# Decode attention over a long key cache: keys transposed as fp32 words, queries computed in row form, and the last output weights loaded in one piece

## The chip, the cores and the metric

One Trainium2 chip, of which one core is used. The time is device microseconds of one execution, the median of several runs. Six runs of the kernel before gave 390.95 to 393.68 us, median 391.86. The profile is of one further execution, which took 392.09 us.

A core has five engines that run their own instruction streams and wait for each other by semaphores: TensorE (PE) for matrix products, its weight loads shown apart as PEld; VectorE (DVE) and ScalarE (ACT) for elementwise work; GpSimd (POOL); and SyncE (SP), which here only issues loads. Sixteen DMA engines move data between the device memory (HBM) and the on-chip buffer. PE writes to PSUM, eight banks of 2 KB in each of 128 partitions, and DVE or ACT copy it out.

## What is computed

Two branches are mixed by a scalar gate. The attention branch takes nearly all of the data: 4 key/value heads with 65,536 keys of 128 numbers, 64 MB of keys and 64 MB of values in bf16, and one query token with 32 heads, 8 for each key head.

```python
q = (x @ wq).reshape(1, 1, 32, 128)                  # x: 1 x 1024, wq: 1024 x 4096
scores = einsum('bhqd,bhkd->bhqk', q, k) * 128 ** -0.5
p = softmax(scores)
a = einsum('bhqk,bhkd->bhqd', p, v).reshape(1, 1, 4096) @ wo    # wo: 4096 x 1024
z = gelu(x @ w_in)                                   # w_in: 1024 x 3584
z1, z2 = z[:1792], layernorm(z[1792:])
b = (z1 * (w_sp * z2 + b_sp)) @ w_out                # w_out: 1792 x 1024
g = sigmoid(sum(x * gate_w))
return g * a + (1 - g) * b
```

## The kernel before

**The program.** `Recorder.op` (L28) notes each operation with its engine, the names it reads and the names it writes; `plan` and `emit` (L54, L93) turn that into waits. Each engine runs its operations in the order in which the code records them. So the order of the code is the order of each queue, and an operation that waits holds up everything behind it on its engine.

**The load stream.** All large inputs go through one ring of five slots of 4 MB (`NS`, L167), issued by SP (`issue`, L330) in one fixed order: wq in two loads, keys 0/1, w_in, keys 2/3, w_in, keys 4/5, w_out, keys 6/7, keys 8/9, values 0/1, keys 10/11, values 2/3 and so on, and at the end wo in six loads (`WO`, L322): three units of 2 MB, then half a unit and two quarters. A load into a slot is issued when `done` (L351) tells that the last reader of what lies there has been recorded; on the chip it then waits for that reader. A "unit" of keys or values is 8192 keys of one head; a load of keys or values holds a pair of units, and partition p holds 128 keys that follow each other. Two small loads, x and gate_w, are issued by ACT.

**The start.** The gate needs x and gate_w: DVE multiplies (L370), PE sums over partitions (L372), ACT and DVE finish it (L374 to L377). The queries follow (L381): 256 matmuls with a 128x128 block of wq as weights and one column of x as the moving operand give q as columns, one per head, in PSUM bank `OB`; four copies (L394) spread them into `qpad`, in which each group of 32 columns for piece j has its 8 queries at columns 8j to 8j+7 and zeros elsewhere.

**Keys.** `k_piece(n, j)` (L403) takes a quarter of unit n: two batches of eight 128x128 bf16 transposes, each batch into one of four PSUM banks, each copied to the `KT` ring of six slots, by DVE (L420) or, for batches 2, 5 and 7 of a unit, by ACT (L417). `s_piece` (L425) follows one piece later with four matmuls of 512 columns that run side by side in four column groups of the array, and accumulates the four pieces into bank `SCB`. After the fourth, DVE copies the scores out with their maximum (L439).

**Values.** After all 8 units of a head, its exponentials are taken (L460, ACT), transposed (`pt_piece`, L464), and multiplied with the values (`pv_piece`, L472, 16 matmuls a unit). So in the middle of the kernel each step handles a key unit and a value unit of nine units earlier. `out_piece` (L490) scales a head's result: it copies bank `OB` to `osb`, computes the factor, and scales `osb` into `osc`.

**Aux work.** The mixer branch lies among the first key units: `win_piece` twice after unit 1 and twice after unit 3, then the layernorm (`mixer_piece`), and `wout_piece` twice after unit 6.

**The end.** For each load of wo, PE multiplies its 8, 4 or 2 rows of 1024 with `ovec` (L623), four matmuls a row; DVE adds the mixer's row (L629), and SP writes the result (L632).

Of the kernel before, what the change touches and what calls it, by code (L numbers as in the profile page):

```python
# [137 lines left out]
def bass_gated_mix__gqa_block_cached__mixer_gmlp__decode_kernel(  # L138
# [22 lines left out]
    KC = D // 128  # L161
# [5 lines left out]
    NS = 5  # L167
    SLOT = 16384
    NB = TILES // 8
    NKTS = 6  # L170
    NSC = 10
    QW = DO // 4
    SCALE = 1.0 / math.sqrt(Dh)
# [13 lines left out]
    for name, n in [  # L187
        ("RING", NS * SLOT), ("KT", NKTS * 1024), ("SC", NSC * 1024), ("PSB", 1024), ("PTSB", 1024),
        ("QPAD", G * 128), ("IDB", 128), ("IDF", 256), ("BM", 256), ("ONES", 256), ("SEL", 16 * 32),
        ("M16", 32), ("M8", 16), ("M32", 64), ("MQ", 32), ("OT", 256), ("XT", KC), ("GW", KC), ("WB", 2), ("MAXC", 2 * G * NU), ("LP", 2 * G * NU),  # L190
        ("COLS", 2 * 64), ("DM", 32), ("OSB", 1024), ("OSC", 512), ("OV", OC), ("Z", 2 * 28), ("Z2", 2 * 28),
        ("ZG", 2 * 28), ("ZE", 2 * 28), ("YB", FC), ("BROW", 2 * QW), ("OROW", QW),
    ]:
        region(name, n)
# [3 lines left out]
    def ab(name, n, o=0):  # L198
        return arena[:, OFF[name] + o:OFF[name] + o + n]

    def af(name, n, o=0):
        return arena[:, OFF[name] + 2 * o:OFF[name] + 2 * (o + n)].bitcast(F32)
# [11 lines left out]
    maxc, lp, colt = af("MAXC", G * NU), af("LP", G * NU), af("COLS", 64)  # L214
    zc, z2, zg, ze = af("Z", 28), af("Z2", 28), af("ZG", 28), af("ZE", 28)
    yb, ovec, orow, brow = ab("YB", FC), ab("OV", OC), ab("OROW", QW), af("BROW", QW)
    osb, osc, dm = af("OSB", 512), ab("OSC", 512), af("DM", 16)
    col = lambda i: colt[:, i:i + 1]
    (C_GS, C_GE, C_G1, C_G, C_OMG, C_MU, C_V, C_S0, C_R0, C_S1, C_R1, C_AL, C_BE, C_T) = range(14)
    C_G4 = 16  # L220
# [1 line left out]
    def gcol(g, i):  # L222
        return col(C_G4 + 11 * g + i)
# [20 lines left out]
    def B(i):  # L244
        return ("bank", i)
# [7 lines left out]
    P("DVE", lambda e: e.memset(ones, 1.0), w=["ones"])  # L253
    P("DVE", lambda e: e.memset(brow, 0.0), w=["brow"])
    P("DVE", lambda e: e.memset(pf(MB), 0.0), w=[B(MB)])


    def small(dst, src, key):
# [15 lines left out]
    def load(keys, pieces):  # L274

        for i, key in enumerate(keys):
            place[key] = (len(stream), i)
        stream.append((keys, pieces))
# [32 lines left out]
    for n in range(NU, total + NU + 1):  # L311
# [7 lines left out]
        else:  # L319
            v = None  # L320
        steps.append((k, v, ()))
    WO = [(0, 0, 8), (1, 0, 8), (2, 0, 8), (3, 0, 4), (3, 4, 6), (3, 6, 8)]  # L322
    for i, c0, c1 in WO:
        load([("wo", i, c0)], [(0, rows(A_wo, i, 8)[:, DO * c0:DO * c1])])

    WIDTH = {"wq": 2 * WQ_N, "win": 2 * F, "wout": 7 * DO, "wo": 8 * DO, "k": UK, "v": UK}
    issued = [0]
# [38 lines left out]
      r=["m32"], w=["sel"])  # L366
    P("DVE", lambda e: e.tensor_reduce(mq, vw(idf, 0, [[1, 16], [16, 8]]), AXX, ALU.add), r=["idf"], w=["mq"])


    P("DVE", lambda e: e.tensor_tensor(z2[:, 0:KC], xT, gw, ALU.mult), r=["xT", "gw"], w=["z2"])  # L370
    P("DVE", lambda e: e.tensor_reduce(col(C_GS), z2[:, 0:KC], AXX, ALU.add), r=["z2"], w=["gs"])  # L371
# [6 lines left out]
      r=["g"], w=["omg"])  # L378


    for i in range(4):  # L381
        sl, key = use(("wq", i))

        def f(e, i=i, sl=sl):
            for k in range(2):
                for h in range(HQ):
                    ins = e.matmul(pf(OB)[:, h:h + 1], sl[:, WQ_N * k + 128 * h:WQ_N * k + 128 * (h + 1)],  # L387
                                   xT[:, 2 * i + k:2 * i + k + 1], start=(i == 0 and k == 0 and h == 0),
                                   stop=(i == 3 and k == 1), skip_group_check=True)
            return ins  # L390
        P("PE", f, r=["xT", key], w=[B(OB)])
        done(("wq", i))
    for g in range(G):
        P("DVE", lambda e, g=g: e.tensor_copy(vw(qpad, 128 * g, [[40, 4], [1, 8]]),  # L394
                                              vw(pf(OB), 8 * g, [[0, 4], [1, 8]])),
          r=[B(OB)], w=["qpad"])


    nbatch = [0]
    pend = []  # L400

    def k_piece(n, j):
        sl, key = use(("k", n))  # L403
        first = nbatch[0]
        for b in (2 * j, 2 * j + 1):
            i = nbatch[0]
            nbatch[0] += 1
            pb = KTB[i % 4]

            def tr(e, b=b, pb=pb):  # L410
                for t in range(8):
                    ins = e.transpose(pbf(pb)[:, 128 * t:128 * (t + 1)],  # L412
                                      sl[:, 128 * (8 * b + t):128 * (8 * b + t + 1)], idb)
                return ins
            P("PE", tr, r=["idb", key], w=[B(pb)])
            if b in (2, 5, 7):
                P("ACT", lambda e, i=i, pb=pb: e.activation(ktb(i), pbf(pb), ACTF.Copy),  # L417
                  w=[("kt", i % NKTS), B(pb)])
            else:
                P("DVE", lambda e, i=i, pb=pb: e.tensor_copy(ktb(i), pbf(pb)), w=[("kt", i % NKTS), B(pb)])  # L420
        if j == 3:
            done(("k", n))
        pend.append((n, j, first))

    def s_piece():  # L425
        if not pend:
            return
        n, j, first = pend.pop(0)
        g, u = KV[n]

        def f(e):
            for cg in range(4):
                src = ktb(first + cg // 2)[:, 512 * (cg % 2):512 * (cg % 2 + 1)]
                ins = e.matmul(pf(SCB)[32 * cg:32 * (cg + 1), :], qpad[:, 128 * g + 32 * j:128 * g + 32 * (j + 1)], src,  # L434
                               start=(j == 0), stop=(j == 3), tile_position=(0, 32 * cg), skip_group_check=True)
            return ins
        P("PE", f, r=["qpad", ("kt", first % NKTS), ("kt", (first + 1) % NKTS)], w=[B(SCB)])
        if j == 3:
            P("DVE", lambda e: e.tensor_scalar(scs(n), pf(SCB), 0.0, None, op0=ALU.add, op1=ALU.max,  # L439
                                               accum_out=maxc[:, n:n + 1]), w=[("sc", n % NSC), ("mx", n), B(SCB)])  # L440
            if u == NU - 1:
                max_piece(g)
# [29 lines left out]
    def pv_piece(n):  # L472
        g, u = KV[n]
        sl, key = use(("v", n))

        def f(e):
            for xi in range(4):
                for cg in range(4):
                    ins = e.matmul(pf(OB)[32 * cg:32 * (cg + 1), :],  # L479
                                   ptsb(n)[:, 128 * xi + 32 * cg:128 * xi + 32 * (cg + 1)],  # L480
                                   vw(sl, 128 * (4 * cg + xi), [[2048, 4], [1, 128]]),
                                   start=(u == 0 and xi == 0), stop=(u == NU - 1 and xi == 3),
                                   tile_position=(0, 32 * cg), skip_group_check=True)
            return ins
        P("PE", f, r=[("ptsb", n % 2), key], w=[B(OB)])
        done(("v", n))
        if u == NU - 1:
            out_piece(g)

    def out_piece(g):  # L490
        P("DVE", lambda e: e.tensor_copy(osb, pf(OB)), w=["osb", B(OB)])
        P("DVE", lambda e: e.tensor_reduce(gcol(g, K_L), lp[:, NU * g:NU * (g + 1)], AXX, ALU.add),
          r=[("lp", NU * g + u) for u in range(NU)], w=[("l", g)])
        P("DVE", lambda e: e.tensor_tensor(gcol(g, K_LW), gcol(g, K_L), gcol(g, K_W), ALU.mult),
# [4 lines left out]
        P("DVE", lambda e: e.scalar_tensor_tensor(gcol(g, K_F), gcol(g, K_RL), gcol(g, K_W), col(C_G),  # L499
                                                  op0=ALU.mult, op1=ALU.mult),  # L500
          r=[("rl", g), ("w", g), "g"], w=[("f", g)])
        P("DVE", lambda e: e.tensor_scalar(osc, osb, gcol(g, K_F), None, op0=ALU.mult),
          r=["osb", ("f", g)], w=["osc"])

        def f(e):
            for c in range(4):
# [86 lines left out]
    for si, (k, v, aux) in enumerate(steps):  # L593
        nxt = steps[si + 1][1] if si + 1 < len(steps) else None
        if k is None and pend:
            s_piece()
        if v is not None and v not in started:
            start_exp(v)
        for j in range(4):
            if k is not None:  # L600
                k_piece(k, j)
                s_piece() if len(pend) > 1 else None
            if j == 1 and v is not None:
                pt_piece(v)
            if j == 2 and nxt is not None and (k is not None or not pend):
                start_exp(nxt)
            if j == 3 and v is not None:
                pv_piece(v)
        if v is not None and v % NU == 0:
            weight_piece(v // NU)  # L610
        for a in aux:
            (win_piece if a[0] == "win" else wout_piece)(a[1])


    FB = KTB[0]
    for i, c0, c1 in WO:
        sl, key = use(("wo", i, c0))

        def f(e, i=i, sl=sl, c0=c0, c1=c1):
            for c in range(c0, c1):  # L620
                for q in range(4):
                    o = DO * (c - c0) + QW * q
                    ins = e.matmul(pf(FB)[32 * q:32 * q + 1, 0:QW], ovec[:, 8 * i + c:8 * i + c + 1],  # L623
                                   sl[:, o:o + QW], start=(i == 0 and c == 0), stop=(i == 3 and c == 7),
                                   tile_position=(0, 32 * q), skip_group_check=True)
            return ins
        P("PE", f, r=[("ovec", i), key], w=[B(FB)])
        done(("wo", i, c0))
    P("DVE", lambda e: e.tensor_tensor(orow[0:97, :], pf(FB)[0:97, 0:QW], brow[0:97, :], ALU.add),  # L629
      r=["brow"], w=["orow", B(FB)])  # L630
    osrc = bass.AP(tensor=arena, offset=OFF["OROW"], ap=[[32 * NA, 4], [1, QW]])
# [31 lines left out]
```

## Time and profile before

| What | Value |
|---|---|
| median of six runs | 391.86 us (390.95 to 393.68) |
| profiled execution, its own time | 392.09 us |
| its span, first to last instruction | 390.2 us |
| PE busy | 276.0 us, 3902 matmuls |
| weight loads busy | 195.9 us, 3902 |
| DVE busy | 160.5 us |
| ACT busy | 124.3 us |
| read from HBM | 162.01 MB, 415 GB/s over the span |
| SP's queue of large loads | 97.2% of 16 engines' span |
| key transposes (L412) | 2048, busy 155.2 us |
| score matmuls (L434) | 512, busy 55.1 us |
| output matmuls (L623) | 128, busy 6.8 us |

Busy time is the union of an engine's instructions; matmuls are pipelined, so a busy PE may still have room. "Idle before" in a group is the time the engine stood still just before it, and the arrow names what ended the wait. DMA share is the mean share of the sixteen DMA engines that were busy; a packet is counted where it ends, so short windows go over 1. The granted clock of TensorE is a share of full speed.

### The profile page before, as it was taken

Reading aid. Unit: us, or ns where it says so; the run is one execution under the profiler, and the core shown is the slowest. Engines: PE = TensorE matmul, PEld = TensorE weight load, DVE = VectorE, ACT = ScalarE, POOL = GpSimd, SP = SyncE. Lnnn points to the kernel's source line nnn. Section 1 sums busy time; section 2 is a strip of 40 time slices with the busy share of each in tenths; the row PEclk is TensorE's granted clock in tenths of the full one; section 3 lists DMA queues with packets and bytes.
Section 4 is the critical chain, followed back from the end, with each engine's and each line's share of the span. In section 5 each row is a group of like instructions: output and inputs, shape, how many; then the busy total and the mean of one; then the engine's idle time right before and its main releaser. Section 6 shows DMA issues by size and latency. Waiting matters only on the chain.

```text
span 390.2 us, 8504 instructions
## 1 busy us (share of the span) xinstructions
PE 276.0 (71%) x3902; PEld 195.9 (50%) x3902; DVE 160.5 (41%) x347; ACT 124.3 (32%) x171; POOL 1.5 (0%) x8
## 2 busy tenths in 40 slices
PE   0000699996999899995789496957993959684463
PEld 0000678885767666664566364735762737321131
DVE  2000043434657665753665263626651635421020
ACT  1000033231546655461346042512560424422000
POOL 1000000000000000000000000000000000000000
PEclk9999998695899999996899798968995888856656
DMA  8999999999999999999999999999999999999993
GB/s 323 430 430 437 422 409 441 426 424 432 405 375 428 428 426 427 428 432 432 424 432 432 428 428 433 432 428 433 430 425 430 432 426 430 428 432 430 420 420 138
DMA packets 7067, 162.56 MB, mean 417 GB/s; under 512 B 1524, under 2 KB 1528, under 8 KB 1784
## 3 DMA queue, kind: packets, MB, share of 16 engines
q1 hardware_dynamic: 6200, 162.01, 97.2%
q8 instruction: 31, 0.51, 0.5%
q10 hardware_dynamic: 832, 0.00, 0.1%
q14 instruction: 4, 0.03, 0.0%
HBM read 162.01 MB, written 0.00 MB: 415 GB/s over the span
## 4 chain that ended last, share of the span: by engine, by line
DMA 52%; PE 38%; DVE 7%; issue 1%; ACT 1%; ACTq 0%; DVEq 0%
DMA arena<-in_A_k_cache_dram 31%; PE pb L412 20%; DMA arena<-in_gate_w_dram 10%; DMA arena<-in_A_v_cache_dram 9%; PE pb L434 6%; PE pb L527 3%; DVE arena L420 3%; PE pb L479 3%; DMA arena<-in_A_wo_dram 2%; PE pb L387 2%; DVE arena L439 2%; PE pb L467 1%; PE pb L623 1%; ACT arena L417 0%; PE pb L575 0%
## 5 line engine op out<-in xcount | busy, mean ns | idle before, releaser
L412 PE MATMUL pb<-arena 128*128 128x128 bf16 x2048 | 155.2, 236 | 32.5 <-DMA arena<-in_A_k_cache_dram 32.1
L412 PEld LDWEIGHTS pb<-arena 128*128 128x128 bf16 x2048 | 133.4, 107 | 61.0 <-DMA arena<-in_A_k_cache_dram 35.2
L420 DVE COPY arena<-pb 128x1024 bf16<-128x1024 bf16 x160 | 108.4, 689 | 113.3 <-PE pb L412 112.6
L417 ACT ACTIVATE arena<-pb 128x1024 bf16<-128x1024 bf16 x96 | 97.9, 1020 | 164.9 <-PE pb L412 164.9
L434 PE MATMUL pb<-arena 128*32 128x512 bf16 x512 | 55.1, 421 | 6.0 <-DVE arena L439 4.0
L479 PE MATMUL pb<-arena 128*32 128x512 bf16 x512 | 39.5, 436 | 13.4 <-DMA arena<-in_A_v_cache_dram 9.0
L372 PE MATMUL pb<-arena 128*128 128x1 f32 x2 | 0.6, 362 | 40.9 <-DVE arena L371 40.9
L479 PEld LDWEIGHTS pb<-arena 128*32 128x32 bf16 x512 | 13.9, 104 | 27.3 <-issue 13.3
L460 ACT ACTIVATE arena<-arena 128x512 bf16<-128x512 f32 x32 | 22.8, 713 | 12.6 <-PE pb L467 10.9
L434 PEld LDWEIGHTS pb<-arena 128*32 128x32 bf16 x512 | 13.3, 93 | 22.8 <-DVE arena L439 7.6
L470 DVE COPY arena<-pb 128x512 bf16<-128x512 bf16 x32 | 13.6, 424 | 27.0 <-PE pb L467 26.7
L439 DVE TENSOR_SCALAR_CACHE_REDUCE arena<-pb 128x512 f32<-128x512 f32 x32 | 21.8, 681 | 2.8 <-PE pb L434 2.8
L372 PEld LDWEIGHTS pb<-arena 128*128 128x128 f32 x2 | 0.5, 310 | 40.9 <-DVE arena L371 40.9
L370 DVE TENSOR_TENSOR arena<-arena 128x8 f32<-128x8 bf16 x1 | 0.2, 169 | 37.2 <-DMA arena<-in_gate_w_dram 37.2
L467 PE MATMUL pb<-arena 128*128 128x128 bf16 x128 | 14.8, 248 | 0.0
L467 PEld LDWEIGHTS pb<-arena 128*128 128x128 bf16 x128 | 8.7, 110 | 11.2 <-issue 10.4
L527 PEld LDWEIGHTS pb<-arena 128*128 128x128 bf16 x224 | 13.6, 161 | 0.5 <-issue 0.5
L527 PE MATMUL pb<-arena 128*128 128x1 bf16 x224 | 13.8, 198 | 0.0
L374 ACT ACTIVATE arena<-pb 128x1 f32<-128x1 f32 x1 | 0.2, 171 | 37.1 <-PE pb L372 37.1
L623 PE MATMUL pb<-arena 128*1 128x256 bf16 x128 | 6.8, 376 | 5.2 <-DMA arena<-in_A_wo_dram 5.1
L387 PE MATMUL pb<-arena 128*128 128x1 bf16 x256 | 7.1, 165 | 2.2 <-issue 2.2
L387 PEld LDWEIGHTS pb<-arena 128*128 128x128 bf16 x256 | 7.2, 105 | 2.2 <-issue 2.2
(78 smaller groups left out, 56.1 us busy)
## 6 DMA issues: line engine op xcount, KB each, us to landing
arena<-in_A_k_cache_dram SPq DMA_DIRECT2D x16, 4096.0 KB, 30.2
arena<-in_A_v_cache_dram SPq DMA_DIRECT2D x16, 4096.0 KB, 31.9
arena<-in_A_wq_dram SPq DMA_DIRECT2D x2, 4096.0 KB, 17.1
arena<-in_B_w_in_dram SPq DMA_DIRECT2D x2, 3584.0 KB, 28.0
arena<-in_A_wo_dram SPq DMA_DIRECT2D x3, 2048.0 KB, 29.4
arena<-in_B_w_out_dram SPq DMA_DIRECT2D x1, 3584.0 KB, 16.9
arena<-in_A_wo_dram SPq DMA_DIRECT2D x1, 1024.0 KB, 21.8
arena<-in_A_wo_dram SPq DMA_DIRECT2D x2, 512.0 KB, 11.4
```

Source lines behind the costliest of these rows:

```text
L387: ins = e.matmul(pf(OB)[:, h:h + 1], sl[:, WQ_N * k + 128 * h:WQ_N * k + 128 * (h + 1)], xT[:, 2 * i + k:2 * i + k + 1], start=(i == 0 and ...
L412: ins = e.transpose(pbf(pb)[:, 128 * t:128 * (t + 1)], sl[:, 128 * (8 * b + t):128 * (8 * b + t + 1)], idb)
L417: P("ACT", lambda e, i=i, pb=pb: e.activation(ktb(i), pbf(pb), ACTF.Copy), w=[("kt", i % NKTS), B(pb)])
L420: P("DVE", lambda e, i=i, pb=pb: e.tensor_copy(ktb(i), pbf(pb)), w=[("kt", i % NKTS), B(pb)])
L434: ins = e.matmul(pf(SCB)[32 * cg:32 * (cg + 1), :], qpad[:, 128 * g + 32 * j:128 * g + 32 * (j + 1)], src, start=(j == 0), stop=(j == 3), ...
L439: P("DVE", lambda e: e.tensor_scalar(scs(n), pf(SCB), 0.0, None, op0=ALU.add, op1=ALU.max, accum_out=maxc[:, n:n + 1]), w=[("sc", n % NSC) ...
L460: P("ACT", lambda e: e.activation(psb(n), scs(n), ACTF.Exp, bias=gcol(g, K_NB), scale=SCALE, accum_out=lp[:, n:n + 1]), r=[("sc", n % NSC) ...
L467: ins = e.transpose(pbf(PTB)[:, 128 * xi:128 * (xi + 1)], psb(n)[:, 128 * xi:128 * (xi + 1)], idb)
L470: P("DVE", lambda e: e.tensor_copy(ptsb(n), pbf(PTB)[:, 0:512]), w=[("ptsb", n % 2), B(PTB)])
L479: ins = e.matmul(pf(OB)[32 * cg:32 * (cg + 1), :], ptsb(n)[:, 128 * xi + 32 * cg:128 * xi + 32 * (cg + 1)], vw(sl, 128 * (4 * cg + xi), [[ ...
L527: ins = e.matmul(pf(MB)[:, z:z + 1], vw(sl, c0, [[FC, 128]]), xT[:, 2 * i + k:2 * i + k + 1], start=(i == 0 and k == 0 and z == 0), stop=( ...
L623: ins = e.matmul(pf(FB)[32 * q:32 * q + 1, 0:QW], ovec[:, 8 * i + c:8 * i + c + 1], sl[:, o:o + QW], start=(i == 0 and c == 0), stop=(i == ...
```

## The change

Three things are altered together.

1. **Keys.** The key slots are read as fp32, each word holding two neighbouring bf16. A 128x128 fp32 transpose puts two keys on each column's partitions: partition 64·par + d/2 holds, for key parity `par`, the words d, d+1. Each batch is four transposes, still a full PSUM bank, and is copied out by the same instructions as before. A score matmul takes every second bf16 of the transposed data (even or odd d), with the queries of even or odd d for one parity as weights; eight of them, over four batches, form one `s_piece`, now twice a unit. `KT` has seven slots.
2. **Queries.** x is padded to `xw`, so that two-column weights (x and a zero) go with 512 moving columns of wq: q comes as rows, in two rows by four column groups of bank `OB`. DVE copies it out as bf16, PE transposes it, and two matmuls with a selection matrix `sele` spread even and odd d over both halves of the partitions; eight copies fill `qpad`. New memsets and copies prepare `xw`, `sele` and the bank. `osb` goes: L502's scaling reads the bank itself.
3. **Output weights.** wo comes in four loads of 2 MB.

The value matmuls take other columns of the slot, to match the new order of the keys (two runs of 256 in place of four of 128).

```diff
-    NKTS = 6
+    NKTS = 7
...
+    P("DVE", lambda e: e.memset(pf(OB), 0.0), w=[B(OB)])
+    P("DVE", lambda e: e.memset(xw, 0.0), w=["xw"])
...
-    WO = [(0, 0, 8), (1, 0, 8), (2, 0, 8), (3, 0, 4), (3, 4, 6), (3, 6, 8)]
-    for i, c0, c1 in WO:
-        load([("wo", i, c0)], [(0, rows(A_wo, i, 8)[:, DO * c0:DO * c1])])
+    for i in range(4):
+        load([("wo", i)], [(0, rows(A_wo, i, 8))])
...
+    for ev in range(2):
+        P("DVE", lambda e, ev=ev: e.tensor_copy(vw(ab("SELE", 128, 128 * ev), 0, [[64, 2], [1, 64]]),
+                                                vw(idb, ev, [[0, 2], [2, 64]])), r=["idb"], w=["sele"])
...
+    P("DVE", lambda e: e.tensor_copy(vw(xw, 1, [[3, KC]]), xT), r=["xT"], w=["xw"])
     for i in range(4):
         sl, key = use(("wq", i))
         def f(e, i=i, sl=sl):
             for k in range(2):
-                for h in range(HQ):
-                    ins = e.matmul(pf(OB)[:, h:h + 1], sl[:, WQ_N * k + 128 * h:WQ_N * k + 128 * (h + 1)],
-                                   xT[:, 2 * i + k:2 * i + k + 1], start=(i == 0 and k == 0 and h == 0),
-                                   stop=(i == 3 and k == 1), skip_group_check=True)
+                c = 2 * i + k
+                for s in range(2):
+                    for cg in range(4):
+                        ins = e.matmul(pf(OB)[32 * cg:32 * cg + 2, :], xw[:, 3 * c + 1 - s:3 * c + 3 - s],
+                                       sl[:, WQ_N * k + 512 * (4 * s + cg):WQ_N * k + 512 * (4 * s + cg + 1)],
+                                       start=(c == 0 and s == 0), stop=(c == KC - 1 and s == 1),
+                                       tile_position=(0, 32 * cg), skip_group_check=True)
...
+    P("DVE", lambda e: e.tensor_copy(qsb[0:98, :], pf(OB)[0:98, :]), w=[("psb", 0), B(OB)])
+    def f(e):
+        for c in range(4):
+            ins = e.transpose(pbf(PTB)[:, 128 * c:128 * c + 98], qsb[0:98, 128 * c:128 * (c + 1)], idb[0:98, 0:98])
+        return ins
+    P("PE", f, r=[("psb", 0), "idb"], w=[B(PTB)])
+    P("DVE", lambda e: e.tensor_copy(vw(qT, 0, [[16, 2], [4, 4], [1, 4]]),
+                                     vw(pbf(PTB), 0, [[1, 2], [32, 4], [128, 4]])), w=["qT", B(PTB)])
+    def f(e):
+        for ev in range(2):
+            ins = e.matmul(pf(PTB)[:, 32 * ev:32 * (ev + 1)], ab("SELE", 128, 128 * ev), qT, start=True, stop=True)
+        return ins
+    P("PE", f, r=["sele", "qT"], w=[B(PTB)])
     for g in range(G):
-        P("DVE", lambda e, g=g: e.tensor_copy(vw(qpad, 128 * g, [[40, 4], [1, 8]]),
-                                              vw(pf(OB), 8 * g, [[0, 4], [1, 8]])),
-          r=[B(OB)], w=["qpad"])
+        for par in range(2):
+            P("DVE", lambda e, g=g, par=par: e.tensor_copy(
+                vw(qpad, 128 * g + 8 * par, [[80, 2], [32, 2], [1, 8]], 64 * par, 64),
+                vw(pf(PTB), 8 * g, [[0, 2], [32, 2], [1, 8]], 64 * par, 64)), r=[B(PTB)], w=["qpad"])
...
     def k_piece(n, j):
         sl, key = use(("k", n))
-        first = nbatch[0]
+        sl = sl.bitcast(F32)
...
             def tr(e, b=b, pb=pb):
-                for t in range(8):
-                    ins = e.transpose(pbf(pb)[:, 128 * t:128 * (t + 1)],
-                                      sl[:, 128 * (8 * b + t):128 * (8 * b + t + 1)], idb)
+                for t in range(4):
+                    ins = e.transpose(pf(pb)[:, 128 * t:128 * (t + 1)],
+                                      sl[:, 128 * (4 * b + t):128 * (4 * b + t + 1)], idf)
...
-        pend.append((n, j, first))
+        if j % 2 == 1:
+            pend.append((n, j // 2, nbatch[0] - 4))
...
     def s_piece():
...
-            for cg in range(4):
-                src = ktb(first + cg // 2)[:, 512 * (cg % 2):512 * (cg % 2 + 1)]
-                ins = e.matmul(pf(SCB)[32 * cg:32 * (cg + 1), :], qpad[:, 128 * g + 32 * j:128 * g + 32 * (j + 1)], src,
-                               start=(j == 0), stop=(j == 3), tile_position=(0, 32 * cg), skip_group_check=True)
+            for ev in range(2):
+                for cg in range(4):
+                    v = 128 * g + 32 * (2 * c + ev)
+                    ins = e.matmul(pf(SCB)[32 * cg:32 * (cg + 1), :], qpad[:, v:v + 32],
+                                   vw(ktb(first + cg), ev, [[2, 512]]), start=(c == 0 and ev == 0),
+                                   stop=(c == 1 and ev == 1), tile_position=(0, 32 * cg), skip_group_check=True)
...
-                                   vw(sl, 128 * (4 * cg + xi), [[2048, 4], [1, 128]]),
+                                   vw(sl, 128 * (8 * cg + 2 * xi), [[4096, 2], [1, 256]]),
...
     def out_piece(g):
-        P("DVE", lambda e: e.tensor_copy(osb, pf(OB)), w=["osb", B(OB)])
...
-        P("DVE", lambda e: e.tensor_scalar(osc, osb, gcol(g, K_F), None, op0=ALU.mult),
-          r=["osb", ("f", g)], w=["osc"])
+        P("DVE", lambda e: e.tensor_scalar(osc, pf(OB), gcol(g, K_F), None, op0=ALU.mult),
+          r=[("f", g)], w=["osc", B(OB)])
...
             if k is not None:
+                ready = len(pend)
                 k_piece(k, j)
-                s_piece() if len(pend) > 1 else None
+                s_piece() if ready else None
...
-    for i, c0, c1 in WO:
-        sl, key = use(("wo", i, c0))
+    for i in range(4):
+        sl, key = use(("wo", i))
```

## The prediction

> **What bounds the kernel now.** I read the page's first three parts, then the chain of waits, then the windows and SP's issues where the chain pointed. Columns of the page: forty slices of 9.75 us, in tenths; then a queue with packets, MB and share.
>
> ```profile
> PE   0000699996999899995789496957993959684463
> DMA  8999999999999999999999999999999999999993
> ...
> q1 hardware_dynamic: 6200, 162.01, 97.2%
> q8 instruction: 31, 0.51, 0.5%
> ```
>
> PE is full only from 50 to 165 us; DMA is full throughout. The chain of waits (start, us, what) is PE's until 154.85 us, from there mostly loads, and it ends:
>
> ```profile
> 333.63 33.79 DMA arena<-in_A_v_cache_dram
> ...
> 377.56 9.48 DMA arena<-in_A_wo_dram
> 387.09 0.62 PE pb L623 x8
> ```
>
> So the end is the load stream plus what PE does after the last landing. PE matters only where it frees a ring slot too late. SP's issues show the one place:
>
> ```profile
> 90.39 0.33 SPq L339 DMA_DIRECT2D arena<-in_A_v_cache_dram  x1
> 107.50 0.33 SPq L339 DMA_DIRECT2D arena<-in_A_k_cache_dram  x1
> ```
>
> and so do half-microsecond windows (last columns: clock, DMA share, GB/s):
>
> ```profile
> 107.50:108.00 0.50, 0.50 (x9) 0.27 (x7) 0.25 (x1) 0.49 (x1) 0.00 (x0) 1.00 0.00 0
> 108.00:108.50 0.50, 0.50 (x13) 0.50 (x11) 0.11 (x1) 0.50 (x1) 0.00 (x0) 1.00 0.77 197
> ```
>
> Keys 10/11 could be issued only when PE had transposed unit 5, and the stream ran dry.
>
> The load before it raises its semaphore sixteen times, once for each DMA engine: the trace's landing records have the first at 106.9 and the last at 109.0 us. Full 4 MB loads follow each other by 9.7 us, so keys 10/11 should have landed at 116.6 to 118.7. They landed at 119.2 to 119.6 (one engine at 121.5): the leading engines lost 2.6 us, the late ones 0.8. At the end the spread is larger: the last piece landed from 381.6 to 387.0. That is why the DMA share falls long before it is over:
>
> ```profile
> 380.00:380.50 0.50, 0.00 (x0) 0.00 (x0) 0.00 (x0) 0.00 (x0) 0.00 (x0) 1.00 1.01 418
> ...
> 384.00:384.50 0.50, 0.00 (x0) 0.00 (x0) 0.00 (x0) 0.00 (x0) 0.00 (x0) 0.50 0.46 188
> ```
>
> About seven of sixteen engines work alone for the last microseconds. What made them late are the packets of q8: 31 of 16 KB, 0.93 to 1.1 us of one engine each. 0.51 MB over PE's 7804 instructions is 65 bytes each, and the other engines have some hundreds. So these are PE's program, and each packet puts one engine back. The landing records show it in rounds over about eight engines: behind the leader by about 2 us at 160, 4 at 250, 5.5 at 367, so some 1.5 us a hit.
>
> **The change, part by part.**
>
> *Last output weights as one load.* The bytes are the same, so the last landing doesn't move: the units and pieces landed at 382.1, 384.6, 385.8 and 387.0, full pace to the end. But PE then has 32 matmuls (L623) to do instead of 8. Two prices stand in the timeline of the tail (start, us):
>
> ```profile
> 375.64 3.58 PE L623 MATMUL pb<-arena 128*1 128x256 bf16 x64
> ...
> 382.16 1.04 PE L623 MATMUL pb<-arena 128*1 128x256 bf16 x32 [2.94 <-DMA arena<-in_A_wo_dram]
> ...
> 387.09 0.59 PE L623 MATMUL pb<-arena 128*1 128x256 bf16 x8 [0.65 <-DMA arena<-in_A_wo_dram]
> ```
>
> At clock 0.5 each group of four takes 3.58/16 = 0.224, so 32 take 8 x 0.224 + 0.145 = 1.93 us: +1.34 over the 0.59. At clock 1.0 it is 1.04: +0.45. The 1.0 came after a busy 376 to 379; before 387 PE will have been idle for nearly four microseconds with one short burst, and the clock was 0.5 there. I take **+1.34**, bounds +0.45 and +1.34. Two SP issues fewer cost nothing: they waited behind L479 and L623 while the queue still held megabytes.
>
> *Keys as fp32 words.* 2048 transposes become 1024, a group of eight bf16 ones (a bank) becomes four fp32 ones. bf16: 16 in 1.00 us at full clock (0.50 a bank), 1.87 at half (0.94). An fp32 128x128 transpose isn't in the trace. Nearest rows, the fp32 products with the same weight shape (ns min/median/max):
>
> ```profile
> L452 PEld LDWEIGHTS pb<-arena x8: 186/189/337, 134.5 to 344.5; 128*128 128x128 f32 x8
> ...
> L412 PEld LDWEIGHTS pb<-arena x2048: 95/98/292, 50.5 to 333.3; 128*128 128x128 bf16 x187
> ```
>
> A call gives two fp32 loads, 0.30 us together at full clock and 0.50 at half (L496), so the second starts 0.30 - 0.186 = 0.114 or 0.50 - 0.333 = 0.167 after the first. From below, four at the bf16 pace: 0.25 a bank. From above, each transpose as a whole fp32 call (0.38 us, L496 at full clock): 1.52. Between: one pass each, at the spacing of the fp32 loads, 4 x 0.114 = **0.46** (0.67 at half clock); or two passes, 0.91. I take 0.46, because the 128 moving columns (62 ns a bf16 transpose) fit beside a 0.114 load.
>
> The Trainium skill ("TensorE: Matmul & The Clock Gate", Weight-path perf modes) speaks against the change: the fast weight load is off for FP32. The fp32 rows above, twice the bf16 ones, agree. By the page's 107 ns for 128 columns (LDWEIGHTS) a bank would be an estimated 0.43 us. Its Terms say that the transpose mode makes FP32 four times faster; no run here shows that.
>
> The evictions (L420, 0.69; L417, 1.02) move the same bytes and stay. Scores are as many, 4 in 0.33 to 0.40 us at full clock, but read every second bf16. No row has a strided moving operand; contiguous (L479) is the lower bound, twice the time the upper (+1.33 us a unit; L527's strided weight loads run at 61 ns against 28 for L387's contiguous ones). I take the lower, since a column still is one element. The chunk of eight waits for four evictions, made one piece earlier; seven KT slots hold four waiting and two being written. Behind a late one PE's next transposes queue, as they do now (L417, 1.9 us in all).
>
> *Queries in row form.* Before, 256 matmuls from 41.38 to 50.64, 2.16 of it "issue". After, xw comes behind L377 on DVE, so PE starts at about 42.5; 64 matmuls of 512 columns, four abreast, 0.43 a group at half clock (L479's 1.90 for 16): 16 x 0.43 = 6.9, to 49.4. Then a chain in which PE waits: drain 0.17, cast 0.69 (as L491), four transposes 0.61 (as L507), copy 0.18, two matmuls 0.31, hops 0.15: 2.1, to 51.5. That is +0.9 before unit 0's transposes; at full clock the groups would take half, 3.5 us less: the lower bound. Behind it queue all of PE's key transposes, and so the slots. The eight qpad copies (0.12 apart in L394, 1.0 us) lie beside transposes. The extra memsets and copies on DVE lie in its 37.2 us wait for gate_w; without that cover they would be about 1.2 us.
>
> *Slot for keys 10/11.* Units 0 to 5 took 12.6, 13.4 and 12.8 us by pairs. After, a pair at full clock is 8 x (2 x 0.46 + 0.40) = 10.6; three pieces at half clock after each run of L527 add 1.6. The first pair follows dense matmuls, so I take it at full clock: 10.6, 12.2, 12.2, a gain of 3.8, less 0.9. The issue comes at 104.6 in place of 107.5. Issue at 107.5 acted as a landing at 109.5, so 104.9 is soon enough for the leading engines and about 106.9 for the late ones: the stall goes. Next in line, values 2/3, is free earlier too.
>
> *PE's program.* 2048 + 384 instructions fewer, about 12 more: 5384; at 65 bytes that is 0.35 MB, 21 packets for 31.
>
> *osb.* One 0.69 copy a group less, before loads that land later anyhow (L623 waited 2.94 after 379.2): nothing.
>
> *Sum.* The leading engines ended at 381.6; without the 2.6 stall 379.0. 21 hits over eight engines are three on the worst, 5.4 behind as after three rounds now: 384.4, against 387.0. So -2.6, +1.34: **-1.26 us**. The profiled execution took 392.09 (span 390.2), 0.23 over the median of 391.86; 392.09 - 1.26 = 390.83, as a median 390.6. Its own range: one hit more or less on the worst engine (1.5) and the warm tail (-0.9), 389.4 to 392.
>
> **Rivals.**
> 1. *PE becomes late: slower.* A bank of fp32 transposes costs more, or strided scores do. For: the doubled fp32 loads, two instructions a call. Against: a transpose needs no sum. 48 banks precede the slot and about 2.3 us are to spare, so it decides from 0.51 a bank. With load and columns one after the other (0.65) the issue is 9.1 later, 113.7, and late engines wait 6.8 in place of 0.8: -1.8 (fetches) + 6.0 + 1.34 = +5.5, 397. Doubled scores: 8 later, +4.4, 396. Two passes (0.91): 21.6 later, about +18, 410, with a pair near 19.8 us of PE against 19.4 of loads ever after.
> 2. *Only the stall's 0.8 us comes back*, because fetches fall on other engines or cost as much. -0.8 + 1.34: 392.4, no change that a measurement tells.
> 3. *The stream is no shorter* (another slot binds or fetches keep their rhythm) and the tail is longer: 393.2, just slower.
>
> **How the numbers follow.** Forecast 0.50, rivals 0.22, 0.20, 0.08. A measurement tells about 0.3%, 1.2 us, from no change. The forecast lies at that edge; its uncertainties (warm tail, two hits) lie more on the fast side: 0.40 faster, 0.10 same. Rival 2 adds 0.17 to same, 0.03 to slower; rivals 1 and 3 are slower. Faster 0.40, same 0.27, slower 0.33. Range 389.3 to 397: it leaves out rival 1's dear end and little below.
>
> **What would show it.** q8 with 21 packets; no window of DMA share near 0 at 100 to 110; keys 10/11 issued before 105; four fp32 transposes in 0.46 us; last landing near 384.4; 32 matmuls in 1.9 us behind it. A bank above 0.51, or scores above 0.40 for four at full clock, makes it wrong.

## The result, and the profile after

The changed kernel takes 390.44 us (median of 25 runs, 390.24 to 390.65); the kernel before, 391.76 in the runs beside it (390.39 to 393.68). The ratio is 0.9965, 95% interval 0.9956 to 0.9973: 1.3 us faster, a third of a per cent, with an interval that stays clear of 1. 390.6 was predicted. The profiled execution took 390.32, its span 388.5.

The page, with the same rows as before (forty slices in tenths; then queues with packets, MB, share):

```profile
PE   0000689988998997686876676868766849565553
...
DMA  8999999999999999999999999999999999999992
...
q1 hardware_dynamic: 5912, 162.01, 97.4%
q8 instruction: 21, 0.34, 0.4%
```

The DMA row is as full as before: the same 162 MB, at the same pace. What differs is q8, PE's program, 21 packets for 31, and what lies around 107 us. SP's issues, and half-microsecond windows with clock, DMA share and GB/s last:

```profile
85.52 0.33 SPq L341 DMA_DIRECT2D arena<-in_A_v_cache_dram  x1
102.22 0.33 SPq L341 DMA_DIRECT2D arena<-in_A_k_cache_dram  x1
```

```profile
107.00:107.50 0.50, 0.50 (x6) 0.35 (x4) 0.31 (x1) 0.00 (x0) 0.00 (x0) 1.00 0.61 262
107.50:108.00 0.50, 0.50 (x21) 0.42 (x24) 0.38 (x1) 0.37 (x1) 0.00 (x0) 1.00 1.22 524
```

Keys 10/11 are issued 5.3 us earlier and the stream no longer runs dry. They land at 116.6 on the leading DMA engine (the leader, the first of the sixteen to land its share of a load) and at 118.5 on the latest, where it was 119.2 to 121.5. The last weights land from 379.0 to 383.9, where it was 381.6 to 387.0: the leaders gain 2.6 us, the latest 3.1. Then the tail (start, us, matmuls):

```profile
379.17 1.88 PE L653 MATMUL pb<-arena 128*1 128x256 bf16 x32 [3.07 <-DMA arena<-in_A_wo_dram]
...
384.08 1.88 PE L653 MATMUL pb<-arena 128*1 128x256 bf16 x32 [3.04 <-DMA arena<-in_A_wo_dram]
386.01 0.42 DVE L659 TENSOR_TENSOR arena<-pb,arena 97x256 bf16<-97x256 f32 x1 [13.44 <-PE pb L653]
```

32 matmuls in 1.88 us follow the last landing, where 8 took 0.59: 1.29 of the 3.1 is given back.

### The profile page after: what moved, and what is told of

It is laid out like the page before. It is cut to its first block, busy times and chain, and to the rows that moved or that the text cites. A ratio compares the mean times of both kernels' runs of the same rounds, so it can differ in the third digit from the quotient of the medians.

```text
span 388.5 us, 6080 instructions
## 1 busy us (share of the span) xinstructions
PE 261.6 (67%) x2692; PEld 174.3 (45%) x2692; DVE 158.9 (41%) x354; ACT 124.4 (32%) x171; POOL 1.5 (0%) x8
## 4 chain that ended last, share of the span: by engine, by line
DMA 64%; PE 31%; DVE 3%; ACT 1%; issue 1%; ACTq 0%; DVEq 0%
DMA arena<-in_A_k_cache_dram 39%; PE pb L440 16%; DMA arena<-in_gate_w_dram 10%; DMA arena<-in_A_v_cache_dram 8%; DMA arena<-in_A_wo_dram 6%; PE pb L464 5%; PE pb L557 3%; PE pb L510 3%; PE pb L396 1%; DVE arena L448 1%; PE pb L498 1%; ACT arena L445 0%; PE pb L653 0%; PE pb L605 0%; DVE arena L421 0%
## 5 line engine op out<-in xcount | busy, mean ns | idle before, releaser
L440 PE MATMUL pb<-arena 128*128 128x128 f32 x1024 | 147.2, 293 | 47.3 <-DMA arena<-in_A_k_cache_dram 46.7
L440 PEld LDWEIGHTS pb<-arena 128*128 128x128 f32 x1024 | 120.3, 150 | 87.4 <-DMA arena<-in_A_k_cache_dram 50.3
L448 DVE COPY arena<-pb 128x1024 bf16<-128x1024 bf16 x160 | 107.1, 687 | 116.2 <-PE pb L440 114.3
L510 PE MATMUL pb<-arena 128*32 128x512 bf16 x512 | 40.3, 443 | 15.5 <-DMA arena<-in_A_v_cache_dram 11.4
L464 PE MATMUL pb<-arena 128*32 128x512 bf16 x512 | 44.4, 425 | 3.7 <-ACT arena L445 2.0
L510 PEld LDWEIGHTS pb<-arena 128*32 128x32 bf16 x512 | 11.9, 104 | 30.9 <-issue 20.1
L378 PEld LDWEIGHTS pb<-arena 128*128 128x128 f32 x2 | 0.5, 309 | 40.8 <-DVE arena L377 40.8
L464 PEld LDWEIGHTS pb<-arena 128*32 128x32 bf16 x512 | 8.3, 96 | 16.8 <-issue 8.0
L498 PE MATMUL pb<-arena 128*128 128x128 bf16 x128 | 14.1, 241 | 0.0
L557 PEld LDWEIGHTS pb<-arena 128*128 128x128 bf16 x224 | 13.7, 159 | 0.0
L557 PE MATMUL pb<-arena 128*128 128x1 bf16 x224 | 13.7, 198 | 0.0
L498 PEld LDWEIGHTS pb<-arena 128*128 128x128 bf16 x128 | 10.4, 108 | 5.8 <-issue 4.6
L653 PEld LDWEIGHTS pb<-arena 128*1 128x1 bf16 x128 | 3.7, 115 | 10.2 <-DMA arena<-in_A_wo_dram 4.7
L396 PE MATMUL pb<-arena 128*2 128x512 bf16 x64 | 5.5, 518 | 0.9 <-DVE arena L387 0.9
```

The lines of the kernel that those rows point to most:

```text
L396: ins = e.matmul(pf(OB)[32 * cg:32 * cg + 2, :], xw[:, 3 * c + 1 - s:3 * c + 3 - s], sl[:, WQ_N * k + 512 * (4 * s + cg):WQ_N * k + 512 * ...
L440: ins = e.transpose(pf(pb)[:, 128 * t:128 * (t + 1)], sl[:, 128 * (4 * b + t):128 * (4 * b + t + 1)], idf)
L464: ins = e.matmul(pf(SCB)[32 * cg:32 * (cg + 1), :], qpad[:, v:v + 32], vw(ktb(first + cg), ev, [[2, 512]]), start=(c == 0 and ev == 0), st ...
L498: ins = e.transpose(pbf(PTB)[:, 128 * xi:128 * (xi + 1)], psb(n)[:, 128 * xi:128 * (xi + 1)], idb)
L510: ins = e.matmul(pf(OB)[32 * cg:32 * (cg + 1), :], ptsb(n)[:, 128 * xi + 32 * cg:128 * xi + 32 * (cg + 1)], vw(sl, 128 * (8 * cg + 2 * xi) ...
L557: ins = e.matmul(pf(MB)[:, z:z + 1], vw(sl, c0, [[FC, 128]]), xT[:, 2 * i + k:2 * i + k + 1], start=(i == 0 and k == 0 and z == 0), stop=( ...
```

## The experiments

Each ran beside the kernel before, in three series in which that kernel's median was 391.89, 391.86 and 392.29. "Above" and "below" are differences of medians. Those to the changed kernel are to its 390.44, which was not measured again in these series, so a few tenths there mean little. All ratios are to the kernel before. Landings, issues and timelines are those of one profiled execution each.

**The change taken apart: tail.** The last unit in pieces again, all else changed:

```diff
-    for i in range(4):
-        load([("wo", i)], [(0, rows(A_wo, i, 8))])
+    WO = [(0, 0, 8), (1, 0, 8), (2, 0, 8), (3, 0, 4), (3, 4, 6), (3, 6, 8)]
+    for i, c0, c1 in WO:
+        load([("wo", i, c0)], [(0, rows(A_wo, i, 8)[:, DO * c0:DO * c1])])
```

> The changed kernel with the last output unit again as a half and two quarters. Theory (the change paid 1.3 us in its tail, 32 matmuls at half clock, 1.88 us in its trace, in place of 8 in 0.59, and earned it back in the stream): the last landing stays at about 384, 8 matmuls follow it in 0.59, and the time is 1.29 below the changed kernel: 389.15, a ratio to before of 0.993. Rival (the stream's end hangs on how the last unit is cut, so that the gain came from loading it whole): the last landing moves out by the microsecond that the tail gains, and the time stays at 390.4.

Measured: 389.14 us (389.07 to 389.20), ratio 0.993 (0.9915 to 0.9946), 1.30 below the changed kernel. The last landing stays at 384.1, and its timeline ends:

```profile
384.15 0.59 PE L655 MATMUL pb<-arena 128*1 128x256 bf16 x8 [0.64 <-DMA arena<-in_A_wo_dram]
384.80 0.42 DVE L661 TENSOR_TENSOR arena<-pb,arena 97x256 bf16<-97x256 f32 x1 [12.17 <-PE pb L655]
```

So the pieces cost the stream nothing, and loading the unit whole is a loss of 1.3 us inside a change that gains. The same the other way round, in the kernel before:

```diff
-    WO = [(0, 0, 8), (1, 0, 8), (2, 0, 8), (3, 0, 4), (3, 4, 6), (3, 6, 8)]
+    WO = [(0, 0, 8), (1, 0, 8), (2, 0, 8), (3, 0, 8)]
```

> The kernel before with the last output unit loaded whole, the tail's part of the change alone. Theory: the last landing stays at 387, 32 matmuls follow in 1.9 us in place of 0.59, the time goes up by 1.3 from 391.76 to 393.1. Rival (the cut into pieces costs the stream something): the landing comes earlier and the time stays within 0.5 of 391.8.

Measured: 393.27 us (392.03 to 394.50), ratio 1.0035 (1.0019 to 1.0052), 1.4 above. As the theory has it: in the profile, an execution of 394.01, 32 matmuls take 1.88 us behind the last landing, which comes at 387.5.

**Why the tail costs this much.** PE kept busy ahead of the last two units:

```diff
     for i in range(4):
         sl, key = use(("wo", i))
+        if i in (2, 3):
+            def stay(e, i=i):
+                for _ in range(6 if i == 2 else 9):
+                    ins = e.matmul(pf(MB), idb, sel, start=True, stop=True)
+                return ins
+            P("PE", stay, r=["idb", "sel"], w=[B(MB)])
```

> The changed kernel with matmuls of 512 columns that keep PE busy while it waits for the last two units: 6 ahead of the third, 9 ahead of the fourth. Their results are not used. Theory (the tail's 1.88 us is the half clock's): the granted clock is 1.0 at the end, the last 32 matmuls take about 1.04, the time is 0.8 below the changed kernel, 389.6. Rival (the last matmuls are limited by weight loads or PSUM, not by the clock): 1.9 us at either clock, 390.4.

Measured: 389.77 us (389.53 to 389.89), ratio 0.9947 (0.9930 to 0.9964), 0.67 below the changed kernel. The timeline, and a two-microsecond window whose third number from the right is the clock:

```profile
384.14 1.04 PE L660 MATMUL pb<-arena 128*1 128x256 bf16 x32 [1.85 <-DMA arena<-in_A_wo_dram]
```

```profile
384.00:386.00 2.00, 1.04 (x32) 0.70 (x32) 0.42 (x1) 0.00 (x0) 0.00 (x0) 1.00 0.00 0
```

The same 32 matmuls take 1.04 us at clock 1.0 and 1.88 at 0.5. So the half clock is shown to cost 0.84 of the 1.29 that the whole unit adds to the tail; the time fell by 0.67, a little less than the 0.8 expected.

**Queries in row form alone**, in the kernel before: the row matmuls, the copy, the transposes and `qT` of the change, then

```diff
-                                              vw(pf(OB), 8 * g, [[0, 4], [1, 8]])),
-          r=[B(OB)], w=["qpad"])
+                                              vw(qT, 8 * g, [[0, 4], [1, 8]])), r=["qT"], w=["qpad"])
```

> The kernel before with its queries in row form alone: keys in bf16, three pieces at the end. Theory: PE leaves the queries by about 49 us in place of 50.6, a warm clock halves the first transposes, so keys 10/11 are issued at about 104.5 to 105.5, the late engines lose nothing (0.8 us); 384 instructions fewer are one or two packets of 31, which may or may not fall on the worst engine (0 to 1.5 us). So 0.8 to 2 us below before, 389.8 to 391. Rival (the fp32 keys bring all of the gain): no change from 391.76.

Measured: 390.75 us (390.53 to 390.99), ratio 0.9971 (0.9957 to 0.9984), 1.1 below before. The row form alone moves the slot. The first line is the kernel before, the others this run (PE's start, and SP's issue of keys 10/11):

```profile
50.50 3.57 PE L412 MATMUL pb<-arena 128*128 128x128 bf16 x32
```

```profile
42.51 5.55 PE L393 MATMUL pb<-arena 128*2 128x512 bf16 x64 [0.92 <-DVE arena L384]
48.87 0.35 PE L404 MATMUL pb<-arena 98*128 98x98 bf16 x4 [0.81 <-DVE arena L400]
49.05 1.95 PE L429 MATMUL pb<-arena 128*128 128x128 bf16 x32
```

```profile
102.66 0.33 SPq L342 DMA_DIRECT2D arena<-in_A_k_cache_dram  x1
```

Its bf16 keys are issued at 102.66, the fp32 keys of the changed kernel at 102.22. The first 32 transposes take 1.95 us, where they took 3.57 before. In this trace the first record of clock 1.0 stands at 46.5 us, under the row matmuls; in the trace of before it stands at 55.4, after these transposes. So with the row form the clock is up when the keys begin. The time is in the theory's range, but the issue is earlier than its 104.5 to 105.5.

**fp32 keys alone, with the whole last unit**: the changed kernel with the 256 column matmuls of the kernel before, and

```diff
+    P("DVE", lambda e: e.tensor_copy(qT, pf(OB)[:, 0:32]), w=["qT", B(OB)])
```

> The changed kernel with its queries in column form, so fp32 keys with the whole last unit. Theory: queries end at about 50.6 and keys start at half clock, keys 10/11 are issued 2 to 3 us later than 102.2, at 104 to 105.5, which is still soon enough; 372 instructions more are one or two packets: 0 to 1.5 us above the changed kernel, 390.4 to 391.9. Rival (row form brings the gain by the early start): keys 10/11 at 107 or later, a dry stretch, 391.2 or more with the same number of packets on the worst engine.

Measured: 391.17 us (390.56 to 392.69), ratio 0.9986 (0.9968 to 1.0004). The time, 0.73 above the changed kernel, lies in the theory's range and at the edge of the rival's, so it does not decide. In the profile, keys 10/11 go out at 107.04, in the range of the rival: PE's column queries end late, partly because PE waits 3.32 us for nothing that the profile shows ("issue", between the two parts; 2.16 before):

```profile
41.31 6.03 PE L394 MATMUL pb<-arena 128*128 128x1 bf16 x221
50.66 1.07 PE L394 MATMUL pb<-arena 128*128 128x1 bf16 x35 [3.32 <-issue]
```

The profiled execution is the slowest of the twelve, 392.69; when the others issued these keys, no trace shows. Against the kernel before with the whole unit (393.27, 30 packets of PE's program) these keys still bring 2.1 us (22 packets), although the stream runs dry in both profiles.

**PE's program.** Useless instructions, where PE waits for loads anyway:

```diff
+        if si >= 17 and v is not None and v < 30:
+            def idle(e):
+                for _ in range(55):
+                    ins = e.matmul(pf(MB)[0:1, 0:1], idb[:, 0:1], idb[:, 0:1], start=True, stop=True)
+                return ins
+            P("PE", idle, r=["idb"], w=[B(MB)])
```

> The changed kernel with 1210 one-column matmuls added on PE (2420 instructions), 55 behind each value unit from step 17 on, where PE waits for loads anyway. Their results are not used. Theory (each 16 KB packet of PE's program puts one DMA engine back by some 1.5 us, and the engine hit most often sets the end): 30 or 31 packets in the queue of instructions in place of 21, the worst engine one hit more, the last landing at 385.3 to 386 in place of 384, the time 1.3 to 2 us above the changed kernel, 391.7 to 392.4; a slot freed late or a dry stretch of the load stream does not occur. Rival (the program's packets cost nothing that counts, the whole gain was the missing key slot stall): time and last landing as in the changed kernel, 390.4 and 384.

Measured: 392.23 us (391.97 to 393.19), ratio 1.0015 (1.0001 to 1.0028), 1.8 above the changed kernel. Keys 10/11 are issued at 102.87, and the window shares stay at 1.0 until 350 us. The page's queue row, and the tail:

```profile
q8 instruction: 30, 0.49, 0.5%
```

```profile
380.86 1.42 PE L659 MATMUL pb<-arena 128*1 128x256 bf16 x32 [2.33 <-DMA arena<-in_A_wo_dram]
385.81 1.88 PE L659 MATMUL pb<-arena 128*1 128x256 bf16 x32 [3.53 <-DMA arena<-in_A_wo_dram]
```

The leading engine lands the last weights at 379.0, as in the changed kernel; the latest at 385.7 in place of 383.9. So PE's instructions cost time although PE has time: they travel on the engines that carry the data. The landing records say the same packet by packet. Add up how far the sixteen engines are behind the leader: from 125 us on this sum grows by 1.6 to 1.8 us for each packet of q8, in all fourteen traces. So does a pair of runs without a dry stretch and without useless work, both with three pieces at the end: row queries with bf16 keys 390.75, with fp32 keys 389.14. Leaders at 379.1 and 379.2, latest at 385.6 and 384.1. Their packets:

```profile
q8 instruction: 29, 0.48, 0.5%
```

```profile
q8 instruction: 21, 0.34, 0.4%
```

Between these two also lie the seventh `KT` slot, the order of the values and the missing `osb` copy, which were not run alone; the leaders' landings, 0.1 apart, show nothing of them.

**The dry stretch by itself.** PE held up ahead of key unit 4 in the changed kernel, with 22, 45 and 15 matmuls:

```diff
+        if si == 4:
+            def hold(e):
+                for _ in range(22):
+                    ins = e.matmul(pf(MB), idb, sel, start=True, stop=True)
+                return ins
+            P("PE", hold, r=["idb", "sel"], w=[B(MB)])
```

> The changed kernel with 22 matmuls of 512 columns on PE ahead of key unit 4 that hold it up by about 5 us, so that keys 10/11 are issued at about 107.4 us as in the kernel before, and not at 102.2. Their results are not used. Theory (the stall cost the late DMA engines 0.8 us, not the 1.7 to 2.6 that the mean or the leading engine shows, since it lets them catch up): leading engines land keys 10/11 at about 119.1 in place of 116.6, the spread of the sixteen landings shrinks there, and the time is 0.8 above the changed kernel, 391.2. Rival (the stream loses what the leading engine loses): 2.5 above, 392.9.

> The same with 45 such matmuls, about 4.9 us later still: keys 10/11 issued at about 112.3. Theory (from 106.9 on every microsecond of lateness counts in full): 5.4 to 5.7 us above the changed kernel, 395.8 to 396.1, a slope of one against the run with 22. Rival (the ring's slack further on takes some of it up): less than 4 us above.

> The changed kernel with 15 matmuls of 512 columns ahead of key unit 4: with 22 the keys 10/11 were issued at 108.99, so with seven fewer (0.215 each at full clock) at about 107.5, as in the kernel before. Their results are not used. Theory (the end goes by the late DMA engines): the leading engines lose 2.4 to 2.6 us on keys 10/11, the late ones 0.6 to 1, and the median is 0.6 to 1 above the changed kernel, 391.0 to 391.4, with a wide scatter. Rival (the end goes by the leaders' loss): 392.8 to 393.

| matmuls | issue of keys 10/11 | leader's loss on them | latest on last weights | median, range | above the changed kernel |
|---|---|---|---|---|---|
| none | 102.22 | - | 383.9 | 390.44 (390.24 to 390.65) | - |
| 15 | 106.92 | 1.9 | 385.9 | 392.13 (390.29 to 392.85) | 1.7 |
| 22 | 108.99 | 4.0 | 387.8 | 393.05 (391.31 to 394.25) | 2.6 |
| 45 | 113.24 | 8.1 | 391.3 | 396.63 (395.48 to 398.46) | 6.2 |

The ratios are 0.9995 (0.9977 to 1.0013), 1.0030 (1.0011 to 1.0049) and 1.0126 (1.0102 to 1.0149), in the table's order. The three middle columns are of the profiled execution alone; with 22 and 45 it took 394.11 and 397.68, about 1.1 above the median. The hold came out longer than planned with 22, so that run doesn't match the issue time of before; the one with 15 nearly does. The theory in both ("the end goes by the late engines": 0.6 to 1 us) fails: 1.7. The rival's 2.4 to 2.6 was reckoned for an issue at 107.5; at 106.92 the leader lost 1.9, and the median is near that. In the three profiles the span grew by 2.0, 3.8 and 7.4 us, about what the leader lost. From 15 to 45 matmuls the issue moves by 6.3 us and the median by 4.5; the theory's slope of one between 22 and 45 (4.25 later, 3.6 slower) is nearly met. So in the changed kernel a stretch costs about what the leader loses, in the median somewhat less, and it varies from execution to execution: with 15, some took no longer than without.

**Faster versions.** On the changed kernel with three pieces: four pieces, PE kept busy between the landings, and both. `STAY` gives the number of filling matmuls ahead of a piece. These are the lines of the run with both.

```diff
-    WO = [(0, 0, 8), (1, 0, 8), (2, 0, 8), (3, 0, 4), (3, 4, 6), (3, 6, 8)]
+    WO = [(0, 0, 8), (1, 0, 8), (2, 0, 8), (3, 0, 4), (3, 4, 6), (3, 6, 7), (3, 7, 8)]
+    STAY = {(2, 0): 6, (3, 0): 5, (3, 4): 2, (3, 6): 2}
```

> The changed kernel with its last output unit as a half, a quarter and two eighths. Theory: the last landing stays at 384.1, four matmuls follow it, at half clock 0.145 + 0.224 = 0.37 us where eight took 0.59: 0.22 below the run with three pieces (389.14), 388.9. Rival (pieces with 2 KB in each partition move more slowly, or the later issue shows): 389.1 or more.

> The changed kernel with three pieces and with matmuls of 512 columns that keep PE busy between the last landings. Their results are not used. Theory (the clock at the end is 1.0): the last eight take 0.145 + 2 x 0.112 = 0.37 in place of 0.59, 388.9. Rival (the fill-in work itself is in the way when the last piece lands, or the clock is at a half): 389.1 or more.

> Both: four pieces and PE kept busy. Theory: the last four take 0.26, 0.33 below the run with three pieces, 388.8, the fastest of all. Rival (what follows the last landing is by now latency alone): the same as with four pieces.

Measured: 388.99 us, ratio 0.9924 (0.9907 to 0.9941); 388.89, 0.9921 (0.9902 to 0.9939); 388.90, 0.9920 (0.9901 to 0.9938). All beat both kernels; between them, and against three pieces alone (389.14, 0.9930), the intervals tell nothing. With three pieces and a busy PE the last step is as expected:

```profile
384.14 0.39 PE L662 MATMUL pb<-arena 128*1 128x256 bf16 x8 [0.31 <-DMA arena<-in_A_wo_dram]
384.59 0.43 DVE L668 TENSOR_TENSOR arena<-pb,arena 97x256 bf16<-97x256 f32 x1 [12.76 <-PE pb L662]
```

In the profiles with four pieces the last landing is at 384.6 and 384.7, not 384.1, which takes back what the smaller piece saves there. But these two executions, 389.38 each, are the slowest of their runs, 0.4 to 0.5 above the median; whether the others landed as late is not shown.

## Why the prediction was right

The time, the direction and the size (-1.26 forecast, -1.32 measured) held. Step by step:

- **What bounds the kernel**: held. In every profile the span ends 4.5 to 4.6 us after the last landing where a whole unit follows it at half clock, 2.9 to 3.2 with pieces, and 3.7 with a whole unit at full clock.
- **Tail, +1.34**: 1.88 us at half clock for the 1.93 worked out; +1.30 and +1.4 when undone and done alone. The warm bound (1.04) is the one measured with a busy PE.
- **fp32 bank at 0.46**: 0.49 at full clock. Minimum, median and maximum in ns, and two groups of the timeline, at full and at half clock:

```profile
L440 PEld LDWEIGHTS pb<-arena x1024: 137/140/370, 49.3 to 328.6; 128*128 128x128 f32 x171
```

```profile
75.19 1.97 PE L440 MATMUL pb<-arena 128*128 128x128 f32 x16
...
89.64 1.95 PE L440 MATMUL pb<-arena 128*128 128x128 f32 x8
```

16 in 1.97 are four banks, 0.49 each; at half clock 8 in 1.95 are two, 0.98 each, where 0.67 was taken. The half-clock price was wrong by half: a bank costs there what eight bf16 transposes cost (0.94). The fp32 weight load is slower than the bf16 one (median 140 for 98), but not by the factor of two of the fp32 products. The slower load agrees with the Trainium skill ("TensorE: Matmul & The Clock Gate", Weight-path perf modes), by which the fast weight load is off for FP32. Rival 1 falls with the 0.49, by a small margin: it needed 0.51.
- **Strided scores at no extra cost**: held. Eight take 0.65 us at full clock (at 53.16), within the 0.33 to 0.40 for four. Group rows of L464 and, before, L434: mean 425 and 421 ns.

```profile
L464 PE MATMUL pb<-arena 128*32 128x512 bf16 x512 | 44.4, 425 | 3.7 <-ACT arena L445 2.0 <-DVE arena L448 1.7
```

- **Queries, "+0.9 before unit 0's transposes"**: wrong in sign. They start at 49.3, not 51.5, and 1.2 earlier than before:

```profile
42.33 5.49 PE L396 MATMUL pb<-arena 128*2 128x512 bf16 x64 [0.92 <-DVE arena L387]
...
49.32 1.95 PE L440 MATMUL pb<-arena 128*128 128x128 f32 x16
```

The 64 matmuls took 5.49 us for the 6.9, since the clock rose under them: groups of four start 0.43 us apart up to 46.1 and 0.22 apart after it. The chain after them took 1.5 for 2.1.
- **The slot, "a gain of 3.8, less 0.9"**: the issue came at 102.2, not 104.6, and the 3.8 was put down to the wrong part. The row queries alone bring it to 102.66; fp32 keys alone leave it at 107.04 in the one profile, a slow execution. At full clock fp32 banks are no faster (0.49 for 0.50), at half clock neither. What helps is that PE comes to the first keys 1.5 us earlier and at full clock, 1.6 us sooner through 32 transposes (row queries alone). The rest of the 4.8 goes with shorter stretches at half clock further on: by the clock records the next two last 6.8 and 10.2 us there, 10.2 and 13.7 before.
- **The sum, "-2.6, three hits as after three rounds now"**: right in size, as it was booked from leaders and spread, but its parts were misjudged. It gave 2.6 to the stall and nothing to fewer packets. The runs in a row are: before 391.76 to 391.86; row queries 390.75, the stall gone, two packets fewer: -1.0 to -1.1; fp32 keys, eight more packets gone: -1.6; whole last unit: +1.3. So the stall was priced some 1.5 too high and the packets some 1.6 too low, and the two errors cancel: that the time came out within 0.2 is in part luck. Without the stall, 29 packets leave the latest engine 6.5 us behind the leader, 21 leave it 4.9. With the stall gone and the packets as many as before, the spread would not have stayed at 5.4: the stall hid part of the packets' cost. The two don't add up, therefore: in the changed kernel nine packets more cost 1.8 and a stall with nearly the same issue time 1.7, together more than the 2.6 of the stream's whole gain.
- **Rivals 2 and 3** fall with the useless instructions (+1.8 for nine packets) and the row queries alone.

Left open: how much a dry stretch costs an execution, and why it costs less in the kernel before (1.1 with two packets, for 2.6 lost by the leaders) than in the changed one (1.7 for 1.9). The likely account is that the late engines catch up in it and gather their lag anew. The landing records bear out the catching up: the sixteen lags, added up, fall over the load that comes late in all six profiles with a dry stretch (16.0 to 6.7 us before, 9.5 to 8.3 with 15 matmuls) and grow by 1.4 to 1.7 in the eight without. But the lag of the latest engine did not fall before (2.1, then 2.4), and in the kernel before with the whole unit it ended at 7.0, not 5.4. What the catching up is worth at the end is not shown.

## What to carry to other kernels

When loads bind, read the landing of a load engine by engine: the latest sets the end, and what puts it back may be the compute engine's own program. Fewer instructions on an engine that has time can then be worth more than faster ones. And at the end of a stream cut the last load, since what follows its landing is paid in full and may run at a half clock after waiting (32 matmuls in 1.88 us here, 1.04 when PE was kept busy).

## What had not been expected

- With row queries and three pieces at the end, going from 3714 to 2692 matmuls (29 to 21 packets) is worth about 1.6 us, in a kernel in which PE stands idle for about a third of the time.
- Scatter. Kernels whose stream runs dry scatter widely: before 390.39 to 393.68, the whole unit in it 392.03 to 394.50, the run with 15 matmuls 390.29 to 392.85. Those without are mostly tight: 25 runs of the changed kernel within 0.41 us, row queries within 0.46; the useless instructions scatter by 1.2 in the time, but by 0.3 in the span. The queries' 64 matmuls took 5.49, 6.09 and 6.40 us in three profiles of the same code, so PE's timing varies by a microsecond; it seems to show only where a slot hangs on it.
- The clock. The window from 50 to 60 us before prints 1.00, yet the first 32 transposes took 3.57 us there, the half-clock pace (16 in 1.87). The trace's first clock record stands at 55.4, and the printed clock can't be trusted ahead of it. The Trainium skill ("TensorE: Matmul & The Clock Gate", Part 4) says that transposes don't bring up the full clock. This case differs: with column queries and fp32 keys, PE does 24 fp32 transposes and nothing else from 52.1 us on, and they start 0.213 us apart up to 55.1, where that trace's first clock record of 1.0 stands, and 0.109 apart after it. Mixed with other matmuls they also keep 1.00, in the windows from 100 to 170 us before and from 100 to 150 in the changed kernel, at 62 ns for a bf16 and 123 for an fp32 one.
